# A second matmul dealt out by f tile, tap products in natural order, and a second DMA sum in two of three superblocks

## The chip, the cores and the metric

The kernel runs on one core of a Trainium2 chip. The metric is the device time of one execution in microseconds. Four runs of the kernel before gave 754.25, 754.61, 755.16 and 755.72 us; their median is 754.89 us. A profiled execution is one more run of the same program, of which every instruction is on record.

## The reference, cut to what matters

The kernel computes two steps one after the other. The first is a dynamic convolution over 8 sequences of 4096 tokens with 192 channels: every token has, for each of 8 heads, 7 weights of its own, which go through a softmax, and a head's 24 channels are summed over the token and the six before it.

```python
w = exp(weight_gen - max) ; w = w / sum(w)              # [8, 4096, 8 heads, 7 taps]
x_pad = concat([zeros(6 tokens), x], axis=1)
x_unf = x_pad[:, s + k, :]                              # 7 shifted copies of x
out = einsum('bshk,bskhg->bshg', w, x_unf)              # [8, 4096, 192]
```

The second is a two-layer network over the resulting 32768 x 192 matrix, with `w_in` of 192 x 2048 and `w_out` of 2048 x 192:

```python
h = x @ w_in
g = h - np.tanh(h)
return g @ w_out
```

## The kernel before, in words

**Tiles.** The 32768 tokens are cut into NTOT = 32 superblocks of 1024 tokens, numbered n = 0 to 31. Partition p of a superblock holds 8 tokens in a row (J = 8), with the six tokens before them as a halo. The 2048 hidden columns are cut into 16 f tiles of 128. The 192 channels are cut into NC = 3 chunks of R = 64. Because a chunk has 64 rows, every matmul uses one half of TensorE's rows (r = 0 or 1), and two matmuls on different halves run side by side: a "pair".

**Softmax.** ScalarE takes the exponential (`softmax_exp`, L146), VectorE sums over the taps (L160), takes the reciprocal (L169) and scales the exponentials (L199) into `wsm`. In a steady superblock, `softmax_norm` (L171) copies the reciprocals into an unused corner of a PSUM tile (L175) and scales from there.

**Products.** `products` (L205) multiplies x by the weights of one tap at a time, seven instructions (L224) of 128 x 1536 elements on POOL (GpSimd). The results are in bf16 and are laid out by chunk: in each chunk, 64 channels of a token lie side by side. Taps 0, 2 and 4 go to the tile `even`, taps 1, 3 and 5 to `odd`, tap 6 to `last`. Then a DMA from POOL's queue adds `odd` to `even` in place (L241). Superblocks 0 and 1 (PLAIN) do without a DMA sum and leave seven tap groups; 2 to 6 (PART) add only the first two pairs and leave five; the others add all three pairs but for a last piece of 512 columns, and leave four groups for chunks 0 and 1 and five for chunk 2. POOL begins with the products of superblock n + 2 in superblock n, not before VectorE has finished the second subtraction there (the order named "pace").

**Transposes.** `conv_sums` (L260) transposes the groups on TensorE by a matmul against an identity (L277), and adds them up in PSUM as it does so: 24 matmuls for a group of three chunks, each of which loads 64 x 128 products as weights and streams 64 columns. `conv_out` (L288) copies the sum to `convT` in bf16, on ScalarE (L303) for chunks 0 and 1 and on VectorE (L301, a CAST) for chunk 2.

**First matmul.** `gemm1` (L315) makes one f tile of `h` for a superblock: six matmuls of 512 columns (L320) into a PSUM tile `ph`. ScalarE writes its tanh (L333), and VectorE subtracts (L334) and leaves `gt` in bf16. `ph` has three buffers, which the transposes' PSUM tiles `pc` use too.

**Second matmul.** `gemm2` (L345) adds up over the 16 f tiles for one block of 128 tokens, in pairs: r = 0 for block i, r = 1 for block i - 1, 192 columns each (L358), 16 pairs for a block. `obank` holds two sums. ScalarE copies a finished block to `out_sb` (L377), and after eight of them SP stores 768 KB.

**Order.** The order is written out by hand (L475 to L583), one list of instructions for each engine. In superblock n, TensorE makes the f tiles of superblock n two at a time, each two followed by one whole block (16 pairs) of the second matmul of superblock n - 1. In the seventh block, the transposes of chunks 0 and 1 of superblock n + 1 are mixed with the pairs; the transposes of chunk 2 follow in one piece, and then come f tiles 14 and 15. x for superblock n + 3 is loaded by SP early in superblock n, for n = 1 to 6 at its end. Superblock 0 has no second matmul to fill in, and after superblock 31 the last second matmul is done by itself (`gemm2_last`, L386).

Of the kernel before, what the change touches and what calls it, by code (L numbers as in the profile page):

```python
# [16 lines left out]
def kernel(  # L17
# [8 lines left out]
    nc = tc.nc  # L26
# [17 lines left out]
    GC = G // NC  # L44
    NPAIR = K // 2
    ACC = NPAIR * J * D - J * R
    PLAIN = (0, 1)
    PART = (2, 3, 4, 5, 6)
    assert S % TOK == 0 and D % R == 0 and H * GC == R and F % P == 0
# [27 lines left out]
    prods_of = {}  # L77
    conv_of = {}
# [92 lines left out]
    def softmax_norm(n, bank):  # L171

        wsm = softmax_tile()
        zr_v = bank[:, 512 - J * H : 512]
        nc.vector.tensor_copy(zr_v, zr_of[n][:])  # L175
        scale(nc.vector, wsm[:], e_of[n], zr_v)
        wsm_of[n] = (wsm, None, None, None)

    def softmax_norm_ramp(n, bank=None):

        softmax_sum(n)
        wsm = softmax_tile()
        if bank is None:
            softmax_recip(n)
            wsm_of[n] = (wsm, None, e_of[n], zr_of[n])
            return
        zr_v = bank[:, 512 - J * H : 512]
        nc.vector.reciprocal(zr_v, zsum_of[n][:])
        if n == 0:
            scale(nc.vector, wsm[:], e_of[n], zr_v)  # L190
        else:
            zr_of[n] = wgpool.tile([P, J * H], FP32, name="zr")
            nc.vector.tensor_copy(zr_of[n][:], zr_v)
        wsm_v = bank[:, 0 : J * H * K].rearrange("p (j h k) -> p j h k", j=J, h=H)
        scale(nc.vector, wsm_v, e_of[n], zr_v)
        wsm_of[n] = (wsm, wsm_v, None if n == 0 else e_of[n], zr_of.get(n))
# [8 lines left out]
    def products(n, taps=None, sums=None, hooks={}, behind=None):  # L205

        x_t = x_of.pop(n)
        wsm, wsm_v, e_t, zr = wsm_of.pop(n)
        if e_t is not None:
            scale(nc.gpsimd, wsm[:], e_t, zr[:])  # L210

        even = ppool.tile([P, NPAIR, NC, J, H, GC], BF16, name="even")
        odd = ppool.tile([P, NPAIR, NC, J, H, GC], BF16, name="odd")
        last = ppool.tile([P, NC, J, H, GC], BF16, name="last")
        dst = {}
        for i in range(NPAIR):
            dst[2 * i] = even[:, i]
            dst[2 * i + 1] = odd[:, i]
        dst[K - 1] = last[:]
        if -1 in hooks:  # L220
            hooks[-1]()
        for eng, k, j0, j1 in taps or [(nc.gpsimd, k, 0, J) for k in range(K)]:
            w = wsm_v if eng is nc.vector else wsm[:]
            mul = eng.tensor_mul(  # L224
                dst[k][:, :, j0:j1].rearrange("p c j h g -> p j h c g"),
                x_t[:, k + j0 : k + j1, :].rearrange("p j (h c g) -> p j h c g", h=H, c=NC),
                w[:, j0:j1, :, k : k + 1]
                .rearrange("p j h (k o) -> p j h k o", o=1)
                .to_broadcast([P, j1 - j0, H, NC, GC]),
            )  # L230
            if k == 0 and behind is not None:


                order(mul, behind, "pace")
            if j1 == 1:
                first_halo[0] = mul
            if (k, n in PART) in ((3, True), (K - 2, False)) and n not in PLAIN:


                acc = 2 * J * D if n in PART else ACC  # L240
                nc.gpsimd.dma_start(  # L241
                    out=even[:].rearrange("p i c j h g -> p (i c j h g)")[:, 0:acc],
                    in_=odd[:].rearrange("p i c j h g -> p (i c j h g)")[:, 0:acc],
                    accum_op=mybir.AluOpType.add,
                    max_dma_last_dim=4096,
                )
            if k in hooks:
                hooks[k]()

        if n in PLAIN:  # L250
            prods_of[n] = [[dst[k] for k in (sums or range(K))]] * NC
        elif n in PART:
            prods_of[n] = [[dst[4], even[:, 0], even[:, 1], dst[5], last[:]]] * NC
        else:
            groups = [last[:]] + [even[:, i] for i in range(NPAIR)]
            prods_of[n] = [
                groups + ([odd[:, NPAIR - 1]] if c == NC - 1 else []) for c in range(NC)
            ]

    def conv_sums(n, parts, pcs, home=None):  # L260
# [8 lines left out]
        for gi in range(max(len(g) for g in prods)):  # L269
            for chunks, pc in zip(parts, pcs):  # L270
                some = [c for c in chunks if gi < len(prods[c])]
                last = gi == max(len(prods[c]) for c in chunks) - 1
                for c in some:
                    for j in range(JH):
                        col = ((c - chunks[0]) * JH + j) * R
                        for r in range(2):
                            nc.tensor.matmul(  # L277
                                pc[r][:, col : col + R] if home else pc[:, r, col : col + R],
                                lhsT=prods[c][gi][
                                    r * R : (r + 1) * R, c, 2 * j : 2 * j + 2  # L280
                                ].rearrange("p j h g -> p (j h g)"),
# [56 lines left out]
    LEAD = 5  # L338

    FILL, AHEAD = 2, 1  # L340
    LATE = (1, 2, 3, 4, 5, 6)
# [3 lines left out]
    def gemm2(i, f0=0, f1=NFT, between=lambda f: None):  # L345

        ops = []
        for r, blk in ((0, i), (1, i - 1)):
            if not 0 <= blk < LAST:
                continue  # L350
            n, j = divmod(blk, J)
            if r == 0 and f0 == 0:
                half[blk] = obank[blk % 2]
            ops.append((r, n, j, half[blk]))
        for f in range(f0, f1):
            for r, n, j, po in ops:
                col = (j % 2) * HT + (j // 2) * P
                mm = nc.tensor.matmul(  # L358
                    po[:, 0:D],
                    lhsT=g_of[n][f][r * R : (r + 1) * R, col : col + P],  # L360
                    rhs=w_out[r * R : (r + 1) * R, f, :],
                    start=(r == 0 and f == 0),
                    stop=(r == 1 and f == NFT - 1),
                )
                if r == 1 and f == 0 and i in (1, LAST):


                    order(mm, probe[0] if i == 1 else last_act[0], "row tiles in one bank")
            between(f)
        if i > 0 and f1 == NFT:  # L370
            blk = i - 1
            n, j = divmod(blk, J)
            po = half.pop(blk)
            if j == 0:
                out_of[n] = opool.tile([P, J, D], FP32, name="out_sb")
            out_sb = out_of[n]
            last_act[0] = nc.scalar.activation(out=out_sb[:, j, :], in_=po[:, 0:D], func=ACT.Copy)  # L377
            if j == J - 1:
                out_of.pop(n)
                g_of.pop(n)  # L380
                nc.sync.dma_start(
                    out=out[n * TOK : (n + 1) * TOK, :].rearrange("(p j) e -> p j e", p=P),
                    in_=out_sb[:],
                )
# [43 lines left out]
    def w_in_rows(c, f0, f1):  # L428

        src = moe_w_in[c * GC : c * GC + 1, f0:f1]  # L430
        return bass.AP(
            tensor=src.tensor, offset=src.offset, ap=[[G * F, H], [F, GC], [1, f1 - f0]]
        )

    def load_w_in(f0, f1, behind=None):
        for c in range(NC):
            dma = nc.gpsimd.dma_start(out=w_in[0:R, c, f0:f1], in_=w_in_rows(c, f0, f1))
            if c == 0 and behind is not None:
                order(dma, behind, "order of the loads")

    def rest_of_w_in():
        load_w_in(FA, F)
# [6 lines left out]
    load_w_in(0, FA, last_exp[0])  # L449
# [5 lines left out]
            (G_, 6, 0, J),  # L455
            (V, 5, 1, J),
            (V, 4, 2, J),
            (V, 5, 0, 1),
            (V, 4, 0, 2),
            (G_, 0, 0, J),  # L460
            (V, 3, 0, J),
            (V, 2, 0, J),
            (G_, 1, 0, J),
# [10 lines left out]
    for c in range(NC):  # L474
# [5 lines left out]
        taps=[(V, 0, 0, J), (V, 1, 0, J)] + [(G_, k, 0, J) for k in range(2, K)],  # L480
        hooks={4: load_w_out},
# [4 lines left out]
    softmax_norm_ramp(2)  # L486
# [8 lines left out]
    for p in range(J):  # L495
        gemm1(0, 2 * p)
        gemm1(0, 2 * p + 1)


        if p == 3:  # L500
            pcs = []
            sums = conv_sums(1, ((0, 1),), pcs, obank)
        if p == 0:
            softmax_exp(3)
        if 3 <= p <= 6:
            some(sums, (3 if p == 3 else 1) * 4 * JH)
    some(sums, K * 4 * JH)
    conv_out(1, ((0, 1),), pcs)
    conv(1, (2,))

    def out_block(n, p, f0=0, f1=NFT, between=lambda f: None):
        gemm2((n - 1) * J + p, f0, f1, between)

    for n in range(1, NTOT):
        for p in range(J):
            more = n < NTOT - 1
            if more and p == 6:
                break
            gemm1(n, 2 * p)
            ahead = AHEAD if p == 0 and n > 1 else 0  # L520
            if ahead:
                out_block(n, p, 0, ahead)
            gemm1(n, 2 * p + 1)
            if n == 1:

                if p == 0:
                    load_wg(5)
# [25 lines left out]
        if not more:  # L553
            continue
# [63 lines left out]
```

The softmax here doesn't subtract the row's maximum and nothing guards it: scores larger than these inputs give would overflow.

## Time and profile before

| what | value |
|---|---|
| median of 4 runs | 754.89 us |
| the profiled execution | 754.62 us |
| its span, first to last instruction | 752.8 us |
| mean granted TensorE clock | 0.999 |
| a superblock, late (427.55 to 450.04) | 22.49 us |
| a superblock, early (60.00 to 82.78) | 22.78 us |
| DMA traffic | 110.82 MB |

The profile names engines PE (TensorE matmuls), PEld (its weight loads), DVE (VectorE), ACT (ScalarE), POOL (GpSimd) and SP (the queue that issues most DMAs). A line such as `L224 POOL ... x93 | 287.0, 3086 | 13.0 <-DVE gt L334 12.4` reads: 93 instructions of line 224 on POOL, 287.0 us busy in all, 3086 ns for one, 13.0 us of idle time ahead of them, 12.4 of which ended when DVE's `gt` of line 334 was there. A timeline's line gives start, duration, engine, line and operation, and in brackets the idle time before it. Starts of matmuls that overlap are a better measure than their durations.

### The profile page before, as it was taken

Reading aid. Unit: us, or ns where it says so; the run is one execution under the profiler, and the core shown is the slowest. Engines: PE = TensorE matmul, PEld = TensorE weight load, DVE = VectorE, ACT = ScalarE, POOL = GpSimd, SP = SyncE. Lnnn points to the kernel's source line nnn. Section 1 sums busy time; section 2 is a strip of 40 time slices with the busy share of each in tenths; the row PEclk is TensorE's granted clock in tenths of the full one; section 3 lists DMA queues with packets and bytes.
Section 4 is the critical chain, followed back from the end, with each engine's and each line's share of the span. In section 5 each row is a group of like instructions: output and inputs, shape, how many; then the busy total and the mean of one; then the engine's idle time right before and its main releaser. Section 6 shows DMA issues by size and latency. Waiting matters only on the chain.

```text
span 752.8 us, 32359 instructions
## 1 busy us (share of the span) xinstructions
PE 731.9 (97%) x14800; PEld 576.7 (77%) x14800; DVE 695.4 (92%) x740; ACT 625.0 (83%) x840; POOL 670.5 (89%) x264
## 2 busy tenths in 40 slices
PE   3899999999999999999999999999999999999997
PEld 2477877778777878787778777777778777878777
DVE  7999999999999999999999999999999999998893
ACT  3988888888888888888888888888888888888883
POOL 7999999999999999999999999999999999999000
PEclk9999999999999999999999999999999999999999
DMA  8935454465556665555666544666544666542312
GB/s 222 211 86 172 146 155 103 115 186 167 159 153 166 186 182 117 141 154 159 178 186 171 121 131 151 172 185 182 115 129 150 169 186 173 118 116 64 79 45 86
DMA packets 25943, 110.82 MB, mean 147 GB/s; under 512 B 4703, under 2 KB 9551, under 8 KB 21838
## 3 DMA queue, kind: packets, MB, share of 16 engines
q1 hardware_dynamic: 14718, 77.03, 28.5%
q0 software_dynamic: 11088, 31.72, 24.8%
q8 instruction: 115, 1.88, 1.0%
q14 instruction: 22, 0.18, 0.1%
HBM read 54.52 MB, written 25.17 MB: 106 GB/s over the span
## 4 chain that ended last, share of the span: by engine, by line
PE 94%; DVE 3%; DMA 2%; SPq 0%; issue 0%; ACT 0%; DVEq 0%
PE obank L358 44%; PE ph L320 43%; PE pc L277 6%; DVE gt L334 2%; PE po L395 1%; DMA x_t<-zero 1%; DMA x_t<-in_x_dram 1%; DVE odd L224 0%; DVE even L224 0%; SPq L113 0%; ACT convT L295 0%; DVE zr L169 0%; DVE zsum L160 0%; SPq L99 0%; DVE out_sb L409 0%
## 5 line engine op out<-in xcount | busy, mean ns | idle before, releaser
L334 DVE TENSOR_TENSOR gt<-ph,th 128x1024 bf16<-128x1024 f32 x512 | 602.3, 1219 | 33.0 <-ACT th L333 30.1
L333 ACT ACTIVATE th<-ph 128x1024 f32<-128x1024 f32 x512 | 497.3, 1022 | 69.8 <-PE ph L320 68.4
L358 PE MATMUL obank<-w_out,gt 64*128 64x192 bf16 x7936 | 412.2, 243 | 0.4 <-issue 0.4
L358 PEld LDWEIGHTS <-gt 64*128 64x128 bf16 x7936 | 356.5, 94 | 56.3
L320 PE MATMUL ph<-convT,w_in 64*128 64x512 bf16 x3072 | 384.2, 377 | 4.9 <-DVE gt L334 2.9
L224 POOL TENSOR_TENSOR even<-x_t,wsm 128x1536 bf16<-128x1536 f32 x93 | 287.0, 3086 | 13.0 <-DVE gt L334 12.4
L224 POOL TENSOR_TENSOR odd<-x_t,wsm 128x1536 bf16<-128x1536 f32 x93 | 286.7, 3083 | 0.0
L320 PEld LDWEIGHTS <-w_in 64*128 64x128 bf16 x3072 | 173.9, 94 | 101.6 <-issue 13.3
L377 ACT ACTIVATE out_sb<-obank 128x192 f32<-128x192 f32 x248 | 82.0, 331 | 35.1 <-PE obank L358 30.8
L224 POOL TENSOR_TENSOR last<-x_t,wsm 128x1536 bf16<-128x1536 f32 x32 | 106.6, 3332 | 0.4 <-DMA x_t<-in_x_dram 0.4
L277 PE MATMUL pc<-ident,even 64*128 64x64 bf16 x2256 | 62.7, 191 | 0.3 <-DVE even L224 0.2
L277 PEld LDWEIGHTS <-even 64*128 64x128 bf16 x2304 | 59.7, 96 | 1.5 <-issue 0.7
L241 POOL DMA_DIRECT2D even<-odd x30 | 36.1, 1205 | 9.3 <-POOL odd L224 9.3
L277 PE MATMUL pc<-ident,last 64*128 64x64 bf16 x752 | 27.2, 191 | 9.8 <-POOL last L224 9.5
L303 ACT ACTIVATE convT<-pc 128x1024 bf16<-128x1024 f32 (+1 forms) x33 | 32.7, 993 | 2.7 <-PE pc L277 2.7
L277 PEld LDWEIGHTS <-last 64*128 64x128 bf16 x768 | 23.1, 96 | 10.1 <-POOL last L224 9.5
L160 DVE TENSOR_REDUCE zsum<-e_t 128x32 f32<-128x224 f32 (+1 forms) x61 | 23.6, 387 | 2.9 <-ACT e_t L146 2.9
L146 ACT ACTIVATE e_t<-wg_t 128x448 f32<-128x448 f32 x32 | 18.5, 577 | 7.7 <-DMA wg_t<-in_weight_gen_dram 7.7
L301 DVE CAST convT<-pc 128x512 bf16<-128x512 f32 x30 | 20.7, 689 | 4.3 <-PE pc L277 2.7
L169 DVE RECIPROCAL zr<-zsum 128x32 f32<-128x32 f32 (+1 forms) x58 | 20.3, 349 | 0.0
L199 DVE TENSOR_TENSOR wsm<-e_t,pc 128x448 f32<-128x448 f32 x28 | 17.4, 621 | 2.9
L277 PE MATMUL pc<-ident,odd 64*128 64x64 bf16 x416 | 14.8, 198 | 1.5 <-POOL odd L224 0.8
(29 smaller groups left out, 77.5 us busy)
## 6 DMA issues: line engine op xcount, KB each, us to landing
x_t<-in_x_dram SPq DMA_DIRECT2D x31, 1344.0 KB, 9.3
even<-odd POOLq DMA_DIRECT2D x25, 1024.0 KB, 8.8
out_dram<-out_sb SPq DMA_DIRECT2D x31, 768.0 KB, 6.9
wg_t<-in_weight_gen_dram SPq DMA_DIRECT2D x32, 224.0 KB, 9.9
even<-odd POOLq DMA_DIRECT2D x5, 768.0 KB, 7.0
x_t<-in_x_dram SPq DMA_DIRECT2D x1, 768.0 KB
w_out<-in_moe_w_out_dram POOLq DMA_DIRECT2D x1, 768.0 KB, 8.6
out_dram<-out_sb SPq DMA_DIRECT2D x4, 192.0 KB, 1.9
```

Of the source, the lines that this page charges most:

```text
L160: nc.vector.reduce_sum(out=zsum_of[n][:, j0 * H : j1 * H], in_=e_of[n][:, j0:j1].rearrange("p j h k -> p (j h) k"), axis=AX.X,)
L169: nc.vector.reciprocal(zr_of[n][:, j0 * H : j1 * H], zsum_of[n][:, j0 * H : j1 * H])
L224: mul = eng.tensor_mul(dst[k][:, :, j0:j1].rearrange("p c j h g -> p j h c g"), x_t[:, k + j0 : k + j1, :].rearrange("p j (h c g) -> p j h ...
L241: nc.gpsimd.dma_start(out=even[:].rearrange("p i c j h g -> p (i c j h g)")[:, 0:acc], in_=odd[:].rearrange("p i c j h g -> p (i c j h g)" ...
L277: nc.tensor.matmul(pc[r][:, col : col + R] if home else pc[:, r, col : col + R], lhsT=prods[c][gi][r * R : (r + 1) * R, c, 2 * j : 2 * j + ...
L301: eng.tensor_copy(out, pc[:, :, 0:cols].rearrange("p r (cj t) -> p r cj t", t=R))
L303: last_conv[0] = nc.scalar.activation(out=out, in_=pc[:, :, 0:cols].rearrange("p r (cj t) -> p r cj t", t=R), func=ACT.Copy,)
L320: nc.tensor.matmul(ph[:, r, :], lhsT=w_in[r * R : (r + 1) * R, c, f * P : (f + 1) * P], rhs=convT[r * R : (r + 1) * R, c, :], start=(c == ...
L333: last_act[0] = nc.scalar.activation(out=th[:], in_=ph_f, func=ACT.Tanh)
L334: last_sub[0] = nc.vector.tensor_sub(gt[:], ph_f, th[:])
L358: mm = nc.tensor.matmul(po[:, 0:D], lhsT=g_of[n][f][r * R : (r + 1) * R, col : col + P], rhs=w_out[r * R : (r + 1) * R, f, :], start=(r == ...
L377: last_act[0] = nc.scalar.activation(out=out_sb[:, j, :], in_=po[:, 0:D], func=ACT.Copy)
```

## The change

1. **Products in natural order.** The tiles `even`, `odd` and `last` become one tile `pr` of [128, 7 taps, 8 tokens, 192 channels]. One instruction covers several taps: in a steady superblock taps 0 and 1, then 2 to 5, then 6, on POOL as before. A transpose takes every third channel as its 64 columns, so its weights are read with a step of three elements; the rows of `w_in` are loaded to match.
2. **DMA sums.** From superblock 5 on, one DMA adds taps 3 to 5 to taps 0 to 2, whole, and leaves four groups for every chunk. PART is 2 to 4 now. In superblocks 13, 14, 16, 17, 19, 20, 22, 23, 25, 26, 28, 29 and 31 a second DMA adds the groups 2 and 6 to 0 and 1, which leaves two groups. POOL issues it after the first multiply of the next superblock's products (for 31 at once).
3. **The deal of the second matmul.** Its pairs form one stream (`out_stream`), and a list says how many of them follow each f tile: 4, 12, 0, 16, 0, 16, 0, 16, 0, 6, 10, 6, 10, 8, 8, 16 in a steady superblock. The transposes of chunks 0 and 1 come in one piece after f tile 13, those of chunk 2 after f tile 14 and its eight pairs. Superblock 1 has a list of its own. In superblock 0, the transposes for superblock 1 stand after f tiles 7, 9, 11 and 13.
4. **Softmax.** The sums are taken after f tiles 2 and 5; the reciprocal is one instruction, straight into the PSUM corner, and the scale follows it. Both copies into `convT` are made by ScalarE. Superblock 2's scale moves from POOL to DVE, superblock 1's is copied by ScalarE.
5. **Loads.** x for superblock n + 3 is always loaded behind the subtraction of f tile 7. The "pace" order is gone. The second part of `w_in` is one DMA where it was three.

```diff
-    PART = (2, 3, 4, 5, 6)
+    PART = tuple(range(2,5))
+    TWO_SUMS = tuple([n for n in range(13,NTOT) if n%3])
+    SUM_FIRST = tuple(range(5,32))
...
     def softmax_norm(n, bank):
...
-        nc.vector.tensor_copy(zr_v, zr_of[n][:])
-        scale(nc.vector, wsm[:], e_of[n], zr_v)
+        nc.vector.reciprocal(zr_v, zsum_of[n][:])
+        def finish():
+            scale(nc.vector, wsm[:], e_of[n], zr_v)
...
+    def dma_sum(pr, k0, k1, src0, src1, step=1):
+        nc.gpsimd.dma_start(
+            out=pr[:, k0:k1].rearrange("p k j d -> p k (j d)"),
+            in_=pr[:, src0:src1:step].rearrange("p k j d -> p k (j d)"),
+            accum_op=mybir.AluOpType.add,
+            max_dma_last_dim=2 * J * D,
+        )
...
+        elif n in PART:
+            mul(nc.gpsimd, 0, 2)
+            mul(nc.gpsimd, 2, 4)
+            dma_sum(pr, 0, 2, 2, 4)
+            mul(nc.gpsimd, 4, K)
+            prods_of[n] = parts(4, 5, 6, 0, 1)
         else:
+            mul(nc.gpsimd, 0, 2)
+            second_sum(n - 1)
+            mul(nc.gpsimd, 2, 6)
+            if n in SUM_FIRST:
+                dma_sum(pr, 0, 3, 3, 6)
+            mul(nc.gpsimd, 6, K)
...
+            if n in TWO_SUMS:
+                to_sum[n] = pr
+                prods_of[n] = parts(0, 1)
+            else:
+                prods_of[n] = parts(6, 0, 1, 2)
+            if n == NTOT - 1:
+                second_sum(n)
+    def second_sum(n):
+        if n in to_sum:
+            dma_sum(to_sum.pop(n), 0, 2, 2, K, 4)
...
-                                lhsT=prods[c][gi][
-                                    r * R : (r + 1) * R, c, 2 * j : 2 * j + 2
-                                ].rearrange("p j h g -> p (j h g)"),
+                                lhsT=prods[c][gi][r * R : (r + 1) * R, 2 * j : 2 * j + 2].rearrange(
+                                    "p j (u c) -> p c (j u)", c=NC
+                                )[:, c],
...
+    EARLY, THIRD = ((7, 3), (9, 1), (11, 7)), 13
+    STEADY = dict(pairs=(4, 12, 0, 16, 0, 16, 0, 16, 0, 6, 10, 6, 10, 8, 8, 16), t1=(14, 8), t2=(13, 0), scale=14, sums=(2, 5))
+    FIRST = dict(pairs=(4, 12, 0, 16, 1, 15, 0, 16, 0, 16, 0, 13, 3, 0, 16, 16), t1=(15, 2), t2=(11, 10), scale=15, sums=(1, 2, 3, 4, 8, 10))
+    X_AT = 7
...
+    for n in range(1, NTOT):
...
+        for f in range(NFT):
+            gemm1(n, f)
...
+            elif f == 1:
+                if n + 3 < NTOT:
+                    softmax_exp(n + 3)
+                if n + 4 < NTOT:
+                    load_wg(n + 4)
+                if n < NTOT - 2:
+                    products(n + 2)
...
+            if f == X_AT and n + 3 < NTOT:
+                load_x(n + 3, last_sub[0])
+            done = 0
+            for chunks, at in sorted((((0, 1), plan["t2"]), ((2,), plan["t1"])), key=lambda c: c[1]):
+                if more and at[0] == f:
+                    out_pairs(at[1] - done)
+                    done = at[1]
+                    pc = transposes(n + 1, chunks)
+                    if chunks == (2,) and n + 3 < NTOT:
+                        finish = softmax_norm(n + 3, pc[:, 0])
+            if finish is not None and f >= plan["scale"]:
+                finish()
+                finish = None
+            out_pairs(plan["pairs"][f] - done)
```

## The prediction, made before the changed kernel had run

> **What bounds the kernel now.** I read the busy times first, then the chain of work that ended last, then one steady superblock engine by engine.
>
> ```profile
> PE 731.9 (97%) x14800; PEld 576.7 (77%) x14800; DVE 695.4 (92%) x740; ACT 625.0 (83%) x840; POOL 670.5 (89%) x264
> ```
>
> ```profile
> PE 94%; DVE 3%; DMA 2%; SPq 0%; issue 0%; ACT 0%; DVEq 0%
> PE obank L358 44%; PE ph L320 43%; PE pc L277 6%; DVE gt L334 2%; PE po L395 1%; DMA x_t<-zero 1%; DMA x_t<-in_x_dram 1%; DVE odd L224 0%; DVE even L224 0%; SPq L113 0%; ACT convT L295 0%; DVE zr L169 0%; DVE zsum L160 0%; SPq L99 0%; DVE out_sb L409 0%
> ```
>
> The chain is TensorE almost throughout: second matmul, first matmul, and 6% transposes (L277). The table of stretches for one steady superblock says the same (length, then busy us and instructions of PE, PEld, DVE, ACT, POOL):
>
> ```profile
> 427.55:450.04 22.49, 22.49 (x462) 17.81 (x458) 21.43 (x23) 19.30 (x27) 21.34 (x8) 1.00 0.58 156
> ```
>
> A superblock takes 22.49 us and PE has no gap in it. Its parts add up: 8 x 1.30 us (12 first-layer matmuls, in the chain) + 8 x 1.32 us (32 second-layer matmuls) = 20.96, which leaves 1.53 us for 104 transposes, 14.7 ns each. The timeline of PE has the same price directly:
>
> ```profile
> 442.55 0.53 PE L277 MATMUL pc<-ident,even 64*128 64x64 bf16 x24
> 442.90 0.30 PE L277 MATMUL pc<-ident,odd 64*128 64x64 bf16 x8
> ```
>
> 24 of them from 442.55 to 442.90 are 14.6 ns each. So a transpose left out is worth 14.6 ns, as long as no other engine takes over; and the others are close: DVE 21.4 us, POOL 21.3 us of 22.49.
>
> **What the change does to PE.** The order of the instructions gives 872 transposes fewer, of 3536. Superblocks 5 and 6 go from five groups of 24 to four (48 in all). Twelve later ones go from 104 to 96 (96). The thirteen with two sums go from 104 to 48 (728). 872 x 14.6 ns = **12.7 us**, all on the path: 0.82 us in each superblock with two sums (22.49 to 21.67), 0.12 us in the others (22.37). First and second matmul keep their numbers.
>
> The remaining 2664 transposes load their weights with a step of three elements. No load in the trace is strided. Lower bound of the extra cost: nothing, since a pair of transposes takes 29 ns whatever hides behind it. Upper bound: one column at a time at the pace of a moving column (216 ns for 512 in a pair of first-layer matmuls, so 53 ns for 128 columns, or 107 ns if both row halves queue), +32 to +104 us for 1332 pairs. I take nothing: the nearest rows are loads of the same size, and they hide behind the matmuls. [...] No run here shows a strided load yet.
>
> **POOL.** It multiplies taps and issues the sums. In catch-up it has a period of 21.55 us:
>
> ```profile
> 312.89 3.36 POOL L224 TENSOR_TENSOR last<-x_t,wsm 128x1536 bf16<-128x1536 f32 x1
> 315.76 3.35 POOL L224 TENSOR_TENSOR even<-x_t,wsm 128x1536 bf16<-128x1536 f32 x1
> ...
> 333.67 1.20 POOL L241 DMA_DIRECT2D even<-odd  x1 [0.30 <-POOL odd L224]
> 334.44 3.36 POOL L224 TENSOR_TENSOR last<-x_t,wsm 128x1536 bf16<-128x1536 f32 x1
> ```
>
> 334.44 - 312.89 = 21.55: seven steps of 2.86 us and 1.53 for the sum (0.30 of drain, 1.23 of issue). Now three instructions do seven taps. What an instruction costs by itself: 448 elements took 0.96 and 1.01 us (L199), 1536 took 2.90, so 1.76 ns an element and 0.20 us fixed; four fewer save 0.8 us (bounds: nothing, and 0.8). Superblock without a second sum: 20.75. The second sum costs POOL 1.23 of issue, up to 1.53, and a wait: it stands behind the first multiply of the next superblock and needs the first sum landed. From the first sum's issue to that point POOL does 0.77 + 2.86 + 5.5 = 9.1 us; the first sum moves 1152 KB, and 1024 KB landed in 8.8 us, 768 KB in 7.0, so 9.7. Wait 0.6, say 0.7 (bounds 0 and 1.7: a sum out by the share that the slowest, 12.1 us of 8.4 median, was). Behind it on POOL stand the multiplies of taps 2 to 6.
>
> Two superblocks with and one without: 2 x (20.75 + 1.2 + 0.7) + 20.75 = 66.05 us. PE for the same three: 2 x 21.67 + 22.37 = 65.71, 66.1 with the ring's stalls below. So POOL keeps pace, just. It also has some room: the second sum is issued about 6.5 us into a superblock, lands 7.0 us later, at 13.5, and is read at 17.0 (14 first-layer tiles of 0.65 and 96 pairs of 0.0825). Some 3 us of lag cost nothing. In the first superblocks POOL is no worse than before: its work for superblock 1 starts about 2 us earlier (no scale of 1.04, one weight issue of 0.6 for 1.70) and for 2 about 3.6, while the first reading moves up by about 3. Cost 0 to 1, taken as 0.5.
>
> **DVE, ACT and the ring of three PSUM buffers.** DVE loses the CAST (0.69), two reciprocals of 0.34 and a copy (0.23) and gets one reciprocal of 0.55: 16 x 1.14 + 2 x 0.36 + 0.55 + 0.62 = 20.1 of 21.67. ACT gets the CAST's work (0.60 for 512 columns): 19.9 of 21.67. Both fit, but the ring ties them: a tile's first matmul waits for the subtraction three places back. In the steady pattern that slack is the 0.26 us that DVE waits for ACT:
>
> ```profile
> 427.73 2.35 DVE L334 TENSOR_TENSOR gt<-ph,th 128x1024 bf16<-128x1024 f32 x2 [0.26 <-ACT th L333]
> 430.00 0.38 DVE L160 TENSOR_REDUCE zsum<-e_t 128x32 f32<-128x224 f32 x1
> ```
>
> The reciprocal and scale (1.17 us) now fall between subtractions 14 and 15 where PE has little to hand over, and the two sums (0.36 each) at f = 2 and 5. Followed through by these durations, subtraction 6 of the next superblock ends about 0.2 us after PE could start tile 9. I take 0.2 us for each of the thirteen, **2.6 us**, none where PE has 22.37 (bounds 0 and 0.5: up to 6.5).
>
> **The ramp** (superblock 0) is DVE's: sixteen subtractions in 18.14 us. A scale of 0.62 for superblock 2 moves ahead of them, less a copy of 0.23: +0.4. At its end PE waits 0.79 us for the transposed chunk (L295) and DVE 1.55 for the next tanh; the last transposes now stand at f = 11 and 13, so PE's next tile starts on subtraction 13, about 1.1 us earlier. Net -0.7 (bounds -1.5 and +1).
>
> **DMA and SP.** Thirteen sums of 768 KB more and slightly larger first ones; the DMA share is 0.58. Loads of x go out at f = 7, 9 us before POOL needs them at the latest; the next store and load stand behind in SP's queue with half a superblock to spare. Nothing.
>
> **Sum:** 754.62 (profiled execution; span 752.8 and 1.8 around it) - 12.7 + 2.6 - 0.7 + 0.5 = 744.3. Against the median of 754.89, which is 0.27 above, 744.6; with a little for POOL's waits, **745**.
>
> **Rivals.**
> 1. POOL becomes the bound (ends slower). If the wide multiplies save nothing (21.55) and the second sum costs its full 1.53 with a wait of 1.7, three superblocks take 3 x 21.55 + 2 x 3.2 = 71.1 us, 5.0 more than PE's; over six such cycles 30, less 3 of room, +27: 771. With no saving but 1.2 + 0.7, 68.5, +11: 756. It decides from 66.6 us per three (room used up), and eats the whole gain at about 68.2. For it: POOL's 89%, the drain before every sum. Against: the fixed 0.20 us that 448 elements show.
> 2. The strided load binds (ends slower): 754.9 - 12.7 + 32 = 774 or more. It decides once a pair of loads takes over 29 + 9.5 us/1332 = 36 ns. For it: nothing strided was ever loaded in this trace. Against: PEld is 77% busy without holding anything up.
> 3. The gain goes into the ring: PE's 0.82 us per two-sum superblock turn into waits for DVE, because ACT and DVE have chains of 20 us with fixed lags. Price up to 0.6 more each, 8: 752. For it: both above 90%. Against: no wait of that kind in the steady trace.
> 4. Better than worked out: no ring stall and a ramp gain of 1.5: 741.
>
> **Chances.** Forecast (741 to 749) 0.62; rival 3 (749 to 753) 0.10; rival 1 in its mild form (753 to 758) 0.11, hard form 0.06; rival 2 0.09; below 741 0.02. Runs tell 0.2%, 1.5 us, from no change: faster 0.73, same 0.07, slower 0.20. The range runs from 740 to 758, which leaves 0.17 out.
>
> **What would show it.** Right: about 13,900 matmuls on PE (some records missing), superblocks of 21.7 to 21.9 us and 22.4 in turn, transposes at 14.6 ns, POOL multiplies of two taps near 5.5 us and of four near 10.8. Wrong: POOL without any idle from superblock 16 on and PE waiting for a sum (pr) before L-lines of transposes (rival 1); transposes at 25 ns or more apiece (rival 2); PE waiting for gt or convT more than 0.3 us per superblock (rival 3).

## The result

The changed kernel takes 753.28 us (median of 42 executions, 745.87 to 757.08), the kernel before 754.59 (63 executions, 753.70 to 756.19). The ratio is 0.9977, with a 95% interval of 0.9969 to 0.9985: faster by 0.23%, where the forecast was 745. Three of the 42 executions took 745.9, 747.0 and 747.7 us, close to the forecast; the other 39 took 750.4 to 757.1. The profiled one took 751.89, with a span of 750.1 us (before 752.8). Here and below a ratio leaves out executions more than 1.5% slower than the fastest of the same kernel (one each of the changed kernel, e4 and e10).

The page of the changed kernel, busy times first, then the chain of work that ended last and the DMA issues (size, median us to landing):

```profile
PE 723.5 (96%) x13928; PEld 566.1 (75%) x13928; DVE 664.2 (89%) x655; ACT 638.9 (85%) x872; POOL 668.7 (89%) x150
...
PE 49%; DMA 4%; POOL 4%; issue 1%; ACT 0%; DVE 0%; POOLq 0%; DVEq 0%
PE obank L389 23%; PE ph L354 22%; DMA pr<-pr 4%; POOL pr L236 4%; PE pc L311 2%; PE po L432 1%; ACT th L367 0%; DVE wsm L207 0%; POOL pr L214 0%; ACT convT L337 0%; DVE pc L176 0%; DVE out_sb L446 0%; ACT ot L445 0%; POOLq L214 0%; DVE gt L368 0%
...
pr<-pr POOLq DMA_DIRECT2D x27, 1152.0 KB, 9.7
pr<-pr POOLq DMA_DIRECT2D x16, 768.0 KB, 6.8
```

872 matmuls are gone from PE, and its busy time fell by 8.4 us. But the chain, which was TensorE nearly throughout, now runs through a DMA sum (`pr<-pr`) and through POOL. (The view could follow it back to 309 us only, so its shares do not add up to 100.) A steady superblock without and one with a second sum, then two pieces of the superblock that lost most (length, then busy us and instructions of PE, PEld, DVE, ACT and POOL, granted clock, DMA share, GB/s):

```profile
427.43:449.83 22.40, 22.40 (x410) 17.30 (x408) 20.96 (x22) 19.95 (x29) 22.10 (x7) 1.00 0.79 197
449.83:471.56 21.73, 21.73 (x404) 16.88 (x402) 20.29 (x21) 19.59 (x28) 21.43 (x5) 1.00 0.82 202
591.00:596.28 5.28, 0.00 (x1) 0.03 (x1) 1.55 (x2) 0.50 (x1) 5.28 (x1) 0.80 0.95 214
596.28:600.00 3.72, 3.72 (x60) 2.97 (x62) 0.00 (x0) 1.11 (x2) 3.42 (x3) 0.50 0.12 25
```

PE has no gap in the first two: 22.40 us for 22.49 before, and 21.73 with a second sum. That is the gain that was expected from the transposes. In the third row PE stands still, and in the fourth it works at half its clock.

From one store of a superblock to the next (the store's line in SP's timeline) I get the whole account. With 22.75 us for the early superblocks, 22.40 and 21.73 as the undisturbed lengths, six superblocks are longer, by 10.4 us in all: one takes 29.99 in place of 21.73 (+8.26), the others add 0.13 to 1.28 each (2.2). Undisturbed, the changed kernel would save some 13 us of the profiled execution; 10.4 came back, and 2.7 are left.

The timeline of the changed kernel around the long superblock (start, duration, engine, line, in brackets the idle time before and who ended it; SPq and POOL's DMA_DIRECT2D are issues of transfers):

```profile
573.35 1.28 POOL L214 DMA_DIRECT2D pr<-pr  x1 [0.30 <-POOL pr L236]
574.16 8.97 POOL L236 TENSOR_TENSOR pr<-x_t,wsm 128x1536 bf16<-128x1536 f32 x2
576.77 0.34 SPq L412 DMA_DIRECT2D out_dram<-out_sb  x1
585.22 1.22 POOL L214 DMA_DIRECT2D pr<-pr  x1 [2.08 <-DMA pr<-pr]
585.38 0.33 SPq L114 DMA_DIRECT2D x_t<-in_x_dram  x1
...
596.28 1.04 PE L311 MATMUL pc<-ident,pr 64*128 64x64 bf16 x32 [5.84 <-DMA pr<-pr]
```

The first sum is issued at 573.35. POOL wants to issue the second at 583.14, waits 2.08 us for the first, and issues at 585.22, just as the next x load (1344 KB) goes out. The second sum needs 10.9 us in place of its usual 6.8 and lands by 596.2. PE has been waiting for it since 590.44. With the usual 6.8 us it would have landed at 592.1: 1.7 us of the stop are POOL's lateness, some 4.1 the long sum. The 32 transposes behind the stop take 1.04 us in place of 0.65, and the 8.26 us lost are 5.84 of waiting and 2.4 of slow work.

The clock fell with the stop: 0.80 in the 5.28 us that end with it, 0.50 in the 3.72 us behind it. No single length of a stop decides it in these traces. Six first-layer matmuls need 0.65 us from start to next start at the full clock, and 1.28 behind this stop (from 598.36). In the runs below they needed 1.28 as well behind stops of 2.11 us (e15, at 375.59) and 3.54 us (e16, at 460.31), and 1.27 behind one of 2.75 us (e16, at 600.25); but 0.64 to 0.65 behind stops of 2.21 and 3.51 us (e16, at 670.13 and 531.49) and 3.66 us (e6, at 663.22). Behind the four longer ones whose rows I have, 4.32 and 4.87 us (e15), 6.85 (e10) and 6.97 (e12), it was 1.28 each time.

### The profile page after: what moved, and what is told of

Its sections match the earlier page's. It is cut to its first block, busy times and chain, and to the rows that moved or that the text cites. A ratio compares the mean times of both kernels' runs of the same rounds, so it can differ in the third digit from the quotient of the medians.

```text
span 750.1 us, 30497 instructions
## 1 busy us (share of the span) xinstructions
PE 723.5 (96%) x13928; PEld 566.1 (75%) x13928; DVE 664.2 (89%) x655; ACT 638.9 (85%) x872; POOL 668.7 (89%) x150
## 3 DMA queue, kind: packets, MB, share of 16 engines
q8 instruction: 109, 1.79, 0.9%
## 4 chain that ended last, share of the span: by engine, by line
PE 49%; DMA 4%; POOL 4%; issue 1%; ACT 0%; DVE 0%; POOLq 0%; DVEq 0%
PE obank L389 23%; PE ph L354 22%; DMA pr<-pr 4%; POOL pr L236 4%; PE pc L311 2%; PE po L432 1%; ACT th L367 0%; DVE wsm L207 0%; POOL pr L214 0%; ACT convT L337 0%; DVE pc L176 0%; DVE out_sb L446 0%; ACT ot L445 0%; POOLq L214 0%; DVE gt L368 0%
## 5 line engine op out<-in xcount | busy, mean ns | idle before, releaser
L368 DVE TENSOR_TENSOR gt<-ph,th 128x1024 bf16<-128x1024 f32 x512 | 602.9, 1218 | 66.1 <-ACT th L367 65.6
L236 POOL TENSOR_TENSOR pr<-x_t,wsm 128x3072 bf16<-128x3072 f32 (+3 forms) x95 | 629.8, 6827 | 6.6 <-PE obank L389 4.4
L354 PE MATMUL ph<-convT,w_in 64*128 64x512 bf16 x3072 | 405.4, 378 | 5.6 <-DVE gt L368 3.6
L389 PE MATMUL obank<-w_out,gt 64*128 64x192 bf16 x7936 | 399.3, 243 | 0.2 <-issue 0.2
L408 ACT ACTIVATE out_sb<-obank 128x192 f32<-128x192 f32 x248 | 82.3, 332 | 12.9 <-PE obank L389 10.4
L214 POOL DMA_DIRECT2D pr<-pr x43 | 54.9, 1277 | 20.9 <-DMA pr<-pr 11.1
L311 PEld LDWEIGHTS <-pr 64*128 64x128 bf16 x2664 | 51.8, 102 | 23.8 <-POOL pr L236 10.0
L311 PE MATMUL pc<-ident,pr 64*128 64x64 bf16 x2496 | 50.6, 194 | 16.4 <-POOL pr L236 9.8
L337 ACT ACTIVATE convT<-pc 128x1024 bf16<-128x1024 f32 (+1 forms) x62 | 50.5, 817 | 7.1 <-PE pc L311 6.6
L176 DVE RECIPROCAL pc<-zsum 128x64 f32<-128x64 f32 x28 | 15.4, 550 | 0.0
L432 PE MATMUL po<-w_out,gt 64*128 64x192 bf16 x256 | 11.2, 243 | 0.0
L236 DVE TENSOR_TENSOR pr<-x_t,obank 128x1536 bf16<-128x1536 f32 (+4 forms) x8 | 10.3, 1347 | 0.6 <-ACT wsm L199 0.6
```

Source lines behind the costliest of these rows:

```text
L214: nc.gpsimd.dma_start(out=pr[:, k0:k1].rearrange("p k j d -> p k (j d)"), in_=pr[:, src0:src1:step].rearrange("p k j d -> p k (j d)"), acc ...
L236: return eng.tensor_mul(pr[:, k0:k1, j0:j1, :].rearrange("p k j (h g) -> p k (j h) g", h=H), bass.AP(tensor=x_v.tensor, offset=x_v.offset ...
L311: nc.tensor.matmul(pc[r][:, col : col + R] if home else pc[:, r, col : col + R], lhsT=prods[c][gi][r * R : (r + 1) * R, 2 * j : 2 * j + 2] ...
L337: last_conv[0] = nc.scalar.activation(out=out, in_=pc[:, :, 0:cols].rearrange("p r (cj t) -> p r cj t", t=R), func=ACT.Copy,)
L354: nc.tensor.matmul(ph[:, r, :], lhsT=w_in[r * R : (r + 1) * R, c, f * P : (f + 1) * P], rhs=convT[r * R : (r + 1) * R, c, :], start=(c == ...
L368: last_sub[0] = nc.vector.tensor_sub(gt[:], ph_f, th[:])
```

## The experiments

All changes are to the changed kernel unless said otherwise. Ratios are to the kernel before. My theory from the changed kernel's trace: TensorE's gain is real, and POOL with its sums takes it back. Rivals: the x load that meets the second sum, and something in TensorE's own program.

### e1: no second sum

```diff
-    TWO_SUMS = tuple([n for n in range(13,NTOT) if n%3])
+    TWO_SUMS = ()
```

> No superblock gets a second sum; all from 5 on keep four groups. Theory (POOL falls behind where two of three superblocks have a second sum, until a sum lands late and PE stops): no late stop, every superblock 22.40 us, so 752 us, and the runs lie within 2 us of one another as those of the kernel before do. Rival A (the other parts of the change cost or lose the missing time, the second sums gain as they should): 760 or more, since the gain of 8.7 us by the second sums is taken away from 753. Rival B (the second sums land late because the load of x runs beside them, whatever POOL's pace): 752 as well.

Measured: 762.27 us (759.76 to 765.35), ratio 1.0102 [1.0080, 1.0123]. By its number that is rival A, but its cause is not: superblocks from 11 on should take 22.40 and often took 22.5 to 23.7, 8.9 us more in all, by waits of which the changed kernel has few. TensorE's timeline in this kernel, three of the eight waits (the idle time stands in the brackets):

```profile
291.44 0.37 PE L354 MATMUL ph<-convT,w_in 64*128 64x512 bf16 x1 [0.69 <-issue]
...
383.28 0.37 PE L354 MATMUL ph<-convT,w_in 64*128 64x512 bf16 x1 [0.70 <-issue]
...
565.74 0.37 PE L354 MATMUL ph<-convT,w_in 64*128 64x512 bf16 x1 [0.98 <-issue]
```

They stand at one instruction, by the trace the last matmul of f tile 3, in every second superblock but one, and nothing that the profile shows releases them ("issue"). Two more of this kind stand at second-layer matmuls (284.14 and 375.97). The idle time of the ten adds up to 5.7 us; the rest of the 8.9 shows as no wait of TensorE. The changed kernel has one of them too, 0.69 us at 291.07. So e1 could not serve as the undisturbed reference, and a second cause was on the table.

### e5, e13, e14: TensorE's program moved by 192, 256 and 128 instructions

A superblock with one sum has 448 matmuls, each with its weight load: 896 TensorE instructions, and two of them 1792 = 7 x 256. The instruction queue's row says 109 packets and 1.79 MB for the changed kernel, which has 27,856 TensorE instructions (matmuls and weight loads): 256 for each packet. For the kernel before it says 115 packets, for 29,600 instructions: 257. Cutting some first-layer matmuls in two moves everything behind them; the arithmetic stays the same.

```diff
         for c in range(NC):
+            cuts = (0, 256, HT) if n == 11 else (0, HT)      # e5: +192
+            cuts = (0, 256, HT) if n == 11 or (n == 10 and c == 0) else (0, HT)      # e13: +256
+            cuts = (0, 256, HT) if n == 11 and c < 2 else (0, HT)      # e14: +128
+            for t0, t1 in zip(cuts, cuts[1:]):
```

All three with `TWO_SUMS = ()`.

> The kernel without second sums, whose matmuls of the first layer are cut in two (twice 256 columns) in superblock 11 alone: 192 instructions of TensorE more, 0.2 us, and from superblock 12 on each instruction stands 192 places later in TensorE's program. There a wait of 0.2 to 1.0 us stood at the same instruction (the third f tile of every second superblock, 896 instructions to a superblock). Theory of the place in the program (TensorE waits for instructions at fixed places in its program, which cost more where the transfers are dense): the wait moves to another f tile or goes, and the time changes by some us, 754 to 765. Rival (a collision in the schedule at that f tile): the waits stay at the third f tile of every second superblock, 762.

> One sum everywhere, with cuts in superblocks 10 and 11 that move TensorE's later instructions by 256 places (192 took the waits away, 762 to 753). A superblock has 896 TensorE instructions and the waits stood in every second superblock: 1792 is seven times 256. Theory (instructions reach TensorE in blocks of 256, and a wait arises where a block's border falls on one place of the schedule): a shift by a whole block changes nothing, the waits are back at the first matmul after f tile 2, 760 to 764 us. Rival (any shift, or the cut itself, clears them): 752 to 753.5.

> The same with a shift of 128 places, half a block. Theory: the border falls on the same place of the schedule in the superblocks between: the waits change from the even to the odd superblocks (or back) and remain, 759 to 764 us. Rival (any shift clears them): 752 to 753.5.

Measured: e5 752.89 (751.76 to 755.24), 0.9977 [0.9966, 0.9989], with every superblock from 13 on at 22.40 and no such wait after 270.64. So e5 is the reference that e1 was to be, and it comes near the 752 that the theory gave for e1: without second sums nothing is lost but by these waits. e13 761.86 (760.72 to 764.37), 1.0098 [1.0080, 1.0116]. e14 764.31 (762.57 to 766.26), 1.0122 [1.0104, 1.0140]. The timelines of TensorE, first e13, then e14:

```profile
293.00 0.37 PE L356 MATMUL ph<-convT,w_in 64*128 64x512 bf16 x1 [0.81 <-issue]
...
384.31 0.37 PE L356 MATMUL ph<-convT,w_in 64*128 64x512 bf16 x1 [0.97 <-issue]
```

```profile
314.04 0.37 PE L356 MATMUL ph<-convT,w_in 64*128 64x512 bf16 x1 [0.69 <-issue]
360.12 0.37 PE L356 MATMUL ph<-convT,w_in 64*128 64x512 bf16 x1 [0.69 <-issue]
406.47 0.37 PE L356 MATMUL ph<-convT,w_in 64*128 64x512 bf16 x1 [0.97 <-issue]
```

A shift by 256 leaves them in the superblocks where e1 has them; one by 128 moves them to the superblocks between (314, 360, 406 in place of 291, 337, 383). The traces show the period directly. Take all of TensorE's instructions ahead of such a wait: its matmuls, its weight loads and its own few waiting instructions. In e1, e13 and e14, the count is 193 above a multiple of 256 at each of the 35 waits without a releaser; so it is at the two of the kernel before (0.36 us at 193.42, 0.30 at 217.57) and at the three of the changed kernel (33.53, 291.07 and 548.72). So the waits keep to one place in every 256 of TensorE's instructions. I call it a block border. My reading is that the instructions come in blocks of this length, and that TensorE has run out of them where a border falls on an unlucky place of the schedule. The cost is measured: 9 us between e1 and e5, 1.2%.

### e7: one sum, without x loads from superblock 15 on

```diff
-                load_x(n + 3, last_sub[0])
+                if n + 3 < 15:
+                    load_x(n + 3, last_sub[0])
+                    last_x[0] = x_of[n + 3]
+                else:
+                    x_of[n + 3] = last_x[0]
```

With `TWO_SUMS = ()`.

> The kernel without second sums, and from superblock 15 on without loads of x (x of 14 used again, another output). If the small waits of its late superblocks (22.4 to 23.7 us where 22.40 was expected) come from dense transfers: they go, 753 to 755. If they have to do with the order of PE, DVE and ACT alone: 761 to 763, no change.

Measured: 754.01 (752.39 to 760.83), 0.9996 [0.9977, 1.0016]; all superblocks after 314.61 take 22.40. The block borders stand where e1 has them, yet the waits are gone with the dense transfers. So a border alone is not enough; that the block then comes late, among other transfers, is the likely reading, and no row shows a block's arrival. (But for one in the ramp, e1's waits begin with superblock 11; why not earlier, no run tells.)

### e6: both sums, without x loads from superblock 15 on

The same edit, with the second sums kept.

> As the changed kernel, but from superblock 15 on no x is loaded: the products use the x of superblock 14 again (the output is another from there on). It takes 1344 KB in each superblock away from the DMA engines and leaves POOL's work as it is. Theory (POOL's lag uses up the room, and sums that share the engines with the load of x take 11 us where they would take 7 to 9.7, which adds waits to POOL and makes the last sum late): no stop of PE, 744 to 747 with a spread of 2 us. Rival (lag by POOL's own work alone): a stop all the same, 751 to 753.

Measured: 751.71 (747.40 to 754.40), 0.9961 [0.9946, 0.9977]. The waits of e6 (engine and line, whom it waited for, us in total, times, longest):

```profile
POOL pr L215 <- DMA pr<-pr: 12.4, 7, 6.1
PE pc L312 <- DMA pr<-pr: 5.8, 4, 3.7
```

The rival held: TensorE still waits for sums, four times, up to 3.7 us, though its second sums take only 6.4 to 7.8 us from superblock 13 on. POOL's lateness is enough by itself (its waits for first sums, 0.6 to 1.9 us each up to 631 us, are a part of it); the x load makes a stop longer, it does not make it.

### e3, e15, e16: the x load at other places

```diff
-    X_AT = 7
+    X_AT = 9      # e3;  e15: 12;  e16: 4
```

> As the changed kernel, with the load of x behind the subtraction of f tile 9 where it was 7, some 3 us later. Theory (lag first, the load of x only makes it worse): the second sum still comes later and later, the stop comes later or is shorter; 748 to 752. Rival B (the load of x beside the sum is the whole cause): no stop at all, 744 to 746. Rival C (lag alone, the load of x does not matter): 753, no change.

> The changed kernel with x loaded after f tile 12 in place of 7, about 6.5 us later, when a second sum that was issued in time has landed. Theory (of the stop of 5.8 us some 4 come from the x load beside the second sum, which makes it 10.9 us long in place of 6.8): second sums stay near 6.9 us, the stop is 1 to 2 us or none, 745 to 749. Rival (the load then collides with the next first sum, POOL waits for that and the lag comes back): 751 to 755, and POOL's waits for first sums grow beyond 11 us in all.

> The changed kernel with x loaded after f tile 4, about 4 us earlier, so that it lies beside the end of the first sum and is nearly done when the second is issued. Theory (collision with the second sum): the stop is shorter, 746 to 750. Rival (it takes the first sum's share instead, so the second is issued later): 752 to 755, with POOL waiting longer for first sums.

Measured: e3 753.13 (752.43 to 758.78), 0.9994 [0.9979, 1.0010]; e15 774.69 (768.55 to 776.87), 1.0253 [1.0223, 1.0284]; e16 754.16 (751.91 to 759.69), 0.9999 [0.9980, 1.0018]. The waits of e15, then of e16:

```profile
PE pc L311 <- DMA pr<-pr: 21.2, 8, 4.9
POOL pr L214 <- DMA pr<-pr: 20.6, 8, 5.1
POOL pr L236 <- DMA x_t<-zero: 15.3, 3, 6.0
```

```profile
PE pc L311 <- DMA pr<-pr: 12.0, 4, 3.5
POOL pr L214 <- DMA pr<-pr: 9.5, 4, 6.5
```

All three rivals were nearer than the theory: e16 lies within its rival's range, e3 at its rival C (no change), and e15 far above its rival's 755. At 12 the load itself is late for POOL (15.3 us of waits for x), and TensorE's waits for sums add up to 21.2 us. At 9 (e3) every second sum takes 6.5 to 7.3 us, and still POOL waits 13.2 us for sums in eight places, TensorE 5.8 in four. At 4 no stop is longer than 3.5 us, but there are four: second sums have a median of 9.7 us between 300 and 680 us in place of 6.9. I had thought that without the collision the stop would go. It only comes in smaller pieces. My reading is that a stop gives POOL back as much room as it lasts, so short stops come again sooner. None of the four places of the load frees POOL.

### e9: POOL relieved

```diff
+            light = n >= 13 and n % 3 == 0
+            if not light:
+                mul(nc.gpsimd, 6, K)
-            mul(nc.gpsimd, 6, K)
...
-                prods_of[n] = parts(6, 0, 1, 2)
+                prods_of[n] = parts(2 if light else 6, 0, 1, 2)
```

> The changed kernel without POOL's multiply of tap 6 in superblocks 15, 18, 21, 24, 27 and 30; its place among the four groups is taken by group 2 a second time, so TensorE, the DMA sums and the x loads stay as they are (the output differs). Theory: the late stop comes from POOL's pace (66.2 to 67.2 us per three superblocks against TensorE's 65.86). Without 2.9 us of it POOL has 63.4 and waits for nobody's fault but the sums': no stop, 744 to 747 us, every superblock 21.7 or 22.4. Rival (the sums and loads stop TensorE by themselves, whatever POOL does): the stop stays, 751 to 753.

Measured: 747.43 (746.21 to 748.15), 0.9902 [0.9889, 0.9915]. After the ramp TensorE waits for no sum, every granted clock of the page is 9 tenths or more, and what is over 22.40 or 21.73 are small `issue` waits (the longest 1.11 us at 557.88). DMA sums and x loads are all still issued, and only POOL has less to do. So POOL's pace sets the stop; the rival, which gives it to the transfers whatever POOL does, is out. e9 takes away two things at once, though: the lag, and the meeting that the lag leads to (no second sum goes out less than 4.4 us ahead of an x load, where the changed kernel came to 0.16). That the lag stops TensorE without the meeting is shown by e6 and e3.

### e10: the changed kernel, moved by 192 instructions

The edit of e5, with the second sums kept.

> The changed kernel, with the first-layer matmuls of superblock 11 cut into two of 256 columns each, so that every later TensorE instruction stands 192 places further on. Theory (of the 10.4 us given back in the profiled execution 8.3 are the late stop, which POOL sets, and 2.2 small waits at places of TensorE's program): the stop stays, the small waits go or move: 751 to 754. Rival (places of the program set the stop too): 744 to 747.

Measured, eight executions: 743.77, 744.58, 745.63, 747.82 and 752.40, 752.58, 753.38, 755.59; median 750.11, ratio 0.9920 [0.9885, 0.9954]. The program either stops or does not. The profiled execution (755.59) did:

```profile
521.71 0.33 SPq L114 DMA_DIRECT2D x_t<-in_x_dram  x1
...
522.15 1.22 POOL L214 DMA_DIRECT2D pr<-pr  x1 [2.60 <-DMA pr<-pr]
...
533.61 1.04 PE L311 MATMUL pc<-ident,pr 64*128 64x64 bf16 x32 [6.85 <-DMA pr<-pr]
```

It is the same picture as in the changed kernel, three superblocks earlier: POOL waits 2.60 us for the first sum, the second goes out beside the x load and lands after 11.3 us, PE stops for 6.85, and that superblock takes 31.50 us in place of 21.73. Both of my expectations were half right: the stop is not tied to places of the program, but the four executions without it show what the kernel takes when nothing stops, 743.8 to 747.8. Why 4 of 8 escape here and 3 of 42 in the changed kernel, I can't say: no trace of an execution without the stop was taken.

### e2, e8, e11, e4: how many second sums POOL can carry

```diff
-    TWO_SUMS = tuple([n for n in range(13,NTOT) if n%3])
+    TWO_SUMS = tuple(range(14, NTOT, 2))      # e2, nine
+    TWO_SUMS = tuple([n for n in range(12, NTOT) if n % 5 in (0, 2, 4)])      # e8 and e11, twelve
+    TWO_SUMS = tuple(range(13, NTOT))      # e4, nineteen
```

e11 has e5's shift as well.

> A second sum in every other superblock from 14 on, nine in all. Theory: POOL needs 21.1 + 22.5 = 43.6 us for two superblocks and PE 44.1, so POOL does not fall behind: no late stop, 752 - 9 x 0.67 = 746 us, with a narrow spread. Rival A: 755 or more. Rival B (the load of x beside the sum is enough): stops in this kernel too, about two thirds as often, 750 to 753 with a wide spread.

> Second sums in three of five superblocks from 12 on, twelve in all (12, 14, 15, 17, 19, 20, 22, 24, 25, 27, 29, 30). Theory: for five superblocks POOL needs 2 x 21.1 + 3 x 22.5 = 109.7 and PE 2 x 22.40 + 3 x 21.73 = 110.0, so POOL just keeps pace; 745 to 747 without a stop, with single runs of 750 and more where a wait pushes it over. If the balance point lies lower: 750 to 754.

> A second sum in three of five superblocks, with the same cut in superblock 11. Theory: that version's POOL keeps pace (109.6 us per five superblocks against TensorE's 110.0), and of its time some 2 us are small waits at places of the program. If the shift takes them away, 743 to 744.5; if it brings others in, 745.5 to 748. In neither case a stop of several us.

> A second sum in every superblock from 13 on, nineteen in all. Theory: POOL's pace of 22.4 to 22.8 us becomes that of the whole kernel once 3 us of room are used, about six superblocks on, and stops of PE let its clock drop: 755 to 762. Rival A (the missing time is lost elsewhere): 753 - 6 x 0.67 = 749. Rival B: more stops in proportion, 754 to 756.

Measured: e2 747.40 (746.65 to 748.70), 0.9911 [0.9896, 0.9925]; **e8 745.00 (744.13 to 746.73), 0.9871 [0.9854, 0.9888]**, the fastest; e11 745.43 (744.61 to 755.24), 0.9901 [0.9863, 0.9938], where one of six executions has the long time; e4 769.18 (764.62 to 769.73, and one of 1296 at a mean granted clock of 0.63, which no trace explains), 1.0172 [1.0150, 1.0194]. e2 has no stop and lies 1.4 us above the 746 of the theory, e8 lies on the lower end of its range; e11 has a long execution where none was expected, and e4 lies above all three of its expectations. The waits of e8 and of e4:

```profile
POOL pr L214 <- DMA pr<-pr: 5.2, 6, 1.2
...
PE pc L311 <- DMA pr<-pr: 1.1, 1, 1.1
```

```profile
PE pc L311 <- DMA pr<-pr: 21.7, 6, 6.7
POOL pr L214 <- DMA pr<-pr: 16.6, 7, 8.9
```

The balance can be worked out from the changed kernel's rows:

```profile
111.96 1.28 POOL L214 DMA_DIRECT2D pr<-pr  x1 [0.30 <-POOL pr L236]
112.78 19.98 POOL L236 TENSOR_TENSOR pr<-x_t,wsm 128x1536 bf16<-128x1536 f32 x3
133.06 1.30 POOL L214 DMA_DIRECT2D pr<-pr  x1 [0.30 <-POOL pr L236]
...
349.70 1.29 POOL L214 DMA_DIRECT2D pr<-pr  x1 [0.30 <-POOL pr L236]
...
416.05 1.29 POOL L214 DMA_DIRECT2D pr<-pr  x1 [0.30 <-POOL pr L236]
...
482.28 1.29 POOL L214 DMA_DIRECT2D pr<-pr  x1 [0.30 <-POOL pr L236]
...
549.47 1.29 POOL L214 DMA_DIRECT2D pr<-pr  x1 [0.30 <-POOL pr L236]
```

POOL needs 21.10 us for a superblock (sum issues at 111.96 and 133.06) and some 1.5 more with a second sum, as its cycles of three (349.70 to 416.05 to 482.28: 66.2 to 66.4, less 3 x 21.10, by two) give; PE needs 22.40, and 0.67 less with a second sum. They meet at 1.30/2.17 = 0.60 of the superblocks. Two of three is past it, three of five stands on it, and one of two is well within. With twelve in place of thirteen second sums, e8 gains 9.6 us where the changed kernel gains 1.3.

### e12: e8 with three more multiplies on POOL

```diff
             mul(nc.gpsimd, 6, K)
+            if n in (16, 21, 26):
+                mul(nc.gpsimd, 6, K)
```

> A second sum in three of five superblocks, with tap 6 multiplied twice on POOL in superblocks 16, 21 and 26 (same result). Theory: 2.9 us more make POOL's five superblocks 112.4 against TensorE's 110.0; after two or three of them the room is used up and a sum comes late: 749 to 755, with a stop of 3 to 6 us and a low clock behind it after superblock 21. Rival (POOL has idle time to spare, what counts is the number of sums): 744.5 to 746.5.

Measured: 761.53 (757.01 to 763.87), 1.0083 [1.0059, 1.0107]. The stops are back, two of them: superblocks of 30.51 and 30.31 us in place of 21.73, with the clock at 0.65 and 0.80 around the first:

```profile
387.76 1.21 POOL L214 DMA_DIRECT2D pr<-pr  x1 [2.50 <-DMA pr<-pr]
...
398.59 1.04 PE L313 MATMUL pc<-ident,pr 64*128 64x64 bf16 x32 [6.97 <-issue]
```

The profile names no releaser for these two waits, but they are no block borders (their counts are not those of e1), and each ends 0.1 us after a second sum has landed (10.7 us after 387.76). 8.7 us of POOL work cost 16.5 us of time. I had expected 749 to 755 with one stop, since I counted 3 us of room; e8 has less than one multiply to spare.

## Why the prediction was wrong

- **The transposes** were right. 872 went, and undisturbed superblocks take 22.40 and 21.73 us (worked out: 22.37, and 21.67 before stalls). 80 of the strided ones run in the ramp from 53.46 in steps of 14.5 ns. So the strided weights cost no time, and rival 2 is out.
- **The ring** was priced too high: at most 0.06 us for each two-sum superblock, not 0.2, so 0.8 us in place of 2.6. Rival 3 is out. **Ramp and first superblocks** come to 0.0 (the second store leaves at 87.45 us, before at 87.42), for -0.7 and +0.5.
- **POOL's saving** was mis-sized. Four instructions fewer should give 0.8 us. The seven taps took 20.48 us from first start to last end before (312.89 to 333.37) and take 19.98 now: 0.5. In line the instructions overlap, and the fixed 0.20 us that I took from single ones is 0.125 there. The first sum takes 1.12 with its drain, 1.07 before. So the period is 21.10 us, not 20.75.
- **"POOL keeps pace, just"** is the step that failed. Three superblocks take POOL 66.35, 66.23 and 67.19 us in a row in the changed kernel, where I had 66.05, and PE takes 65.86, where I had 66.1. A few tenths of a microsecond turned a small surplus into a debt. I had written that it decides from 66.6 us, and gave the case 0.11 at 756. Two of the three cycles are below 66.6, so the threshold was too high as well: the lag also carried the second sums towards the x load, 5.7 us ahead of it at 359.98, 4.0 at 493.41, 2.9 at 560.75 and 0.16 at 585.22.
- **"Some 3 us of lag cost nothing"** has the right form, but I priced what lies beyond it as lag, one for one. A late sum costs more: the second sum was taken at 7.0 us (6.8 at the median), and took 10.9 beside an x load, which the step **"DMA and SP: Nothing"** left out; and the stop of 5.84 us took 2.4 more at half clock. So the term "a little for POOL's waits", 0.4 us (744.6 to 745), measured 8.3 in the profiled execution.
- **The small waits of TensorE** are in no step of mine. Of the 2.2 us by which five superblocks are longer, 1.7 lie in the two whose waits stand at block borders (291.07 and 548.72), by the count under e14; for the other 0.5 TensorE shows no wait. The trace of before has two such waits, 0.66 us in all.
- **The sum itself**, 744.3, is near what the program takes when it doesn't stop (743.8 to 747.8 in e10, 745.9 to 747.7 in the changed kernel), but that is in part luck: 1.8 us too much for the ring stand against 2.2 of small waits that were left out. Without either the profiled execution would take 741.5 (751.89 less 10.4). The large error is in what was called nothing behind the sum.

What stays open: which small difference decides, from execution to execution, whether the stop comes; and why in e1 the block borders hurt nearly always from superblock 11 on and hardly before.

## What to carry to other kernels

When a change shifts work from the bounding engine to one that is 89% busy, work out both engines' periods for the whole pattern, and set the dose where they still differ by more than the error of the durations: here three of five superblocks gained 9.6 us and two of three 1.3. A lag within the room costs nothing and beyond it costs a stop, with the clock's drop behind a long one (0.50 behind 5.84 us), so price the missed due time, not the lag. Take an instruction's fixed cost from a row where instructions follow one another as they will in the kernel, not from single ones.

## What the runs showed of the hardware

- TensorE's waits without a releaser stand at one count within 256 of its instructions, in e1, e13, e14 and the kernels before and after. Where such a border falls on a bad place and transfers are dense, it waits 0.2 to 1.0 us (up to 1.1 in e9); a shift by 192 instructions was worth 9 us of 762, one by 256 nothing, one by 128 moved the waits to the superblocks between.
- A POOL-issued sum of 768 KB takes 6.8 us at the median, and 10.9 and 11.3 us beside an x load of 1344 KB (changed kernel and e10); one of 1152 KB takes 9.7 at the median and 11.3 just ahead of the stop.
- After a stop of 5.84 us the granted clock was 0.50 for the next 3.7 us; that cost 2.4 us. Shorter stops were uneven: six first-layer matmuls needed 1.28 us behind one of 2.11 us (e15), and 0.65, as at the full clock, behind one of 3.66 (e6).
- Weights read with a step of three elements cost the transposes no time: 14.5 ns a transpose of 64 columns, 14.6 before (a load's own record is 102 ns in the mean, 96 before).
